# A fourth buffer for weight magnitudes, and a list schedule that keeps two engines off one PSUM tile

## The chip, the cores and the metric

The kernel runs on one core of a Trainium2 chip, as one program of 13112 instructions. The metric is the device time of one execution in microseconds (us). The median of three runs of the kernel before is 858.09 us (856.76 to 858.15).

## The reference

Chunked softmax attention, its heads joined to rows of 512, then two feed-forward layers with different activations, all in float32:

```
q, k, v: (4, 8, 576, 64), attention within chunks of 64 positions
attn = softmax(q_c @ k_c^T / 8); x = (attn @ v_c) as (2304, 512)
...
h = x @ w_in                      # layer 1: 512 -> 2048
g = max(h, 0) + log1p(exp(-|h|))  # softplus
x = g @ w_out                     # 2048 -> 512
...
h = x @ w_in2                     # layer 2, the same sizes
P = a0 + a1*h + a2*h^2 + a3*h^3
Q = 1 + |b0|*|h| + |b1|*h^2
out = (P / (Q + 1e-6)) @ w_out2
```

## The kernel before, in words

**Number format.** Each float32 operand of a large product is split into a high and a low part of type fp32r, and a product is three matmuls: high by high, high by low, low by high (`TERMS`). So each weight chunk, each x and each g is made twice, `[0]` high and `[1]` low.

**Tiles.** The 2304 tokens form five blocks (`BLOCKS`, 512 or 384 tokens), run in the order 0, 3, 4, 1, 2 in both layers. The 2048 hidden columns are 16 chunks (`fc`). One block and one chunk are a step `s`: 0 to 79 in layer 1, 80 to 159 in layer 2. A step has 12 matmuls into h (`products_h`, L824), its activation (`softplus`, L862 to L870, or `rational`, L900 to L959), and 12 matmuls in two groups of six into the accumulators (`products_out1`, L992; `products_out2`, L1022). After a block's last step `evacuate` (L1055, L1057) reads the accumulators out.

**Engines.** TensorE (PE) does the matmuls. ScalarE (ACT) does the activations and most high parts, VectorE (DVE) the low parts (L331) and arithmetic, GpSimd (POOL) other low parts (L870, L933). SyncE (SP) issues the transfers.

**Activation tables.** ACT uses one table for exponential, logarithm and Prelu (`EXP_LN`) and another for softplus (`SOFTPLUS`). `table(name)` puts an `ACT_TABLE_LOAD` (L289) into ACT's stream where the set changes.

**The first block.** During steps 0 to 15 the weights of layer 1 are converted. `convert` takes two chunks at a time, one of `w_in` (`wr_1i`, `cm_1i`, `w_1i`) and one of `w_out` (`wr_1o`, `cm_1o`, `w_1o`). `prepare` loads the raw chunk into a buffer of the pool `raw` (4 buffers, L362). ACT makes its magnitude `cm` in a buffer of the pool `cvt` (L380, 3 buffers, Prelu, table `EXP_LN`). DVE shifts it (L389) and merges bits of the raw chunk into it (L395). ACT then takes the high part (L323, no table) and DVE the low part (L331). The softplus of the same steps needs the other table, so a conversion between two steps is a switch there and one back. Meanwhile attention for later tiles runs too: `qk` and `v` are loaded, PE turns them (`qkT`, L572), makes scores, ACT the exponential (`e`, L643; `Exp`, or, where the other table is loaded, softplus of the argument less 20, of which only the ratios matter), PE the values (L696).

**Buffers that the change touches.** The pool `att1` has one buffer per tag. Its tag `v` holds the v of a tile that isn't staged (tiles 4 to 11 and 15 to 17); in layer 2, from step 80 on, it holds the scratch tile `t1` of each third step. PSUM holds two tiles `h`, two `acc`, and `att` for attention, whose room becomes `u0` and `u1` in layer 2 (`square` in `rational`). A tile `h` is read by ACT and DVE, and PE's h two steps later takes its buffer.

**What sets the order.** `Program` is a list scheduler that runs when the kernel is built. Every piece of work is a task (`add`): its engine, an estimated cost, the keys that it reads and writes, the pool tag that it allocates from (`alloc`), the table that it needs. `add` turns keys into dependencies; `alloc` keeps the allocations of one tag in the order in which they were added, and the buffers' release comes from keys with a turn number:

```
def turn(tag, bufs):
    counts[tag] = counts.get(tag, -1) + 1
    return tag, counts[tag] % bufs
```

`forward` plays the engines through in estimated time; where several tasks of an engine are ready, `pick` takes the one with the earliest latest-start time that `backward` gave. `locked` keeps DVE and POOL apart for tasks that both use the memory port. ACT puts off a task that needs the other table, if one that fits is nearly as urgent. `schedule` does this `ROUNDS` = 6 times, three of them with random shifts, and keeps the order that ends first. The tasks' instructions are then issued in that order, on each engine, as written. The costs decide the order only; on the chip each instruction waits for its semaphores.

## Time and profile before

| | |
|---|---|
| three runs, median | 858.09 us (856.76 to 858.15) |
| the profiled execution, its own time | 858.8 us |
| its span | 857.0 us |
| mean granted clock of TensorE | 0.995 |
| PE busy in the span | 842.1 us (98%) |
| DVE, ACT, POOL busy | 641.6, 506.5, 225.6 us |

The span is what the trace covers: from the first instruction to the last. The execution's own time is 1.8 us longer. A row of a timeline gives the start, the time to the end of the last instruction in it, the engine, the line, the operation, the tile written and the tiles read, the shape, how many instructions in a row it groups, and in brackets the idle time before it with what released it. The start of a PE row is recorded; the end is modelled, and so consecutive rows overlap a little. "room" stands for a wait for a buffer to become free.

### The profile page before, as it was taken

The numbers are of one execution on the slowest core, as the hardware profiler recorded it, in microseconds if no ns is written. First come the engines' busy times: TensorE is split into PE (matmuls) and PEld (weight loads), VectorE is DVE, ScalarE is ACT, GpSimd is POOL, SyncE is SP. The second block draws the span as 40 slices with busy tenths as digits, with TensorE's granted clock in tenths as the row PEclk, the third lists the DMA queues.
The fourth block names the chain that finished last, engine by engine and source line by source line (L and its number), as shares of the span: only waits on it lengthen the run. The fifth ranks groups of instructions, "written<-read, shape, count | busy, mean of one in ns | idle before, by whom it ended". The sixth has DMA issues, their size and how long they took to land.

```text
span 857.0 us, 13112 instructions
## 1 busy us (share of the span) xinstructions
PE 842.1 (98%) x5014; PEld 724.1 (84%) x5014; DVE 641.6 (75%) x1119; ACT 506.5 (59%) x875; POOL 225.6 (26%) x206
## 2 busy tenths in 40 slices
PE   7999999999999999999999999999999999999997
PEld 6878779999999888888887888889989888888885
DVE  5766778788899978316776877888878778868774
ACT  4899973233334332344448766767767767756763
POOL 0000002122212222243454821342261352213212
PEclk9899999999999999999999999999999999999999
DMA  9955433413643722235432200200210000001001
GB/s 224 247 181 176 157 99 78 95 39 85 186 123 76 210 75 74 99 119 178 144 116 86 83 1 1 87 0 1 87 50 1 37 1 1 1 0 50 1 1 49
DMA packets 76926, 71.10 MB, mean 83 GB/s; under 512 B 36160, under 2 KB 63808, under 8 KB 76864
## 3 DMA queue, kind: packets, MB, share of 16 engines
q1 hardware_dynamic: 76864, 70.27, 28.5%
q8 instruction: 39, 0.64, 0.3%
q14 instruction: 23, 0.19, 0.1%
HBM read 56.63 MB, written 13.63 MB: 82 GB/s over the span
## 4 chain that ended last, share of the span: by engine, by line
PE 75%; ACT 2%; DVE 2%; issue 0%; POOL 0%; DVEq 0%; POOLq 0%; ACTq 0%
PE h L824 37%; PE acc L1022 22%; PE acc L992 16%; DVE t L903 1%; PE aps L696 1%; ACT t L948 1%; PE aps L606 0%; DVE t L959 0%; ACT t L918 0%; ACT u L922 0%; ACT u L900 0%; ACT u L926 0%; DVE ev L1057 0%; DVE u L903 0%; POOL g L933 0%
## 5 line engine op out<-in xcount | busy, mean ns | idle before, releaser
L824 PE MATMUL h<-xT,w_1i 128*128 128x512 f32 (+1 forms) x960 | 211.1, 370 | 2.3 <-ACT w_1i L323 2.2
L992 PE MATMUL acc<-g,w_1o 128*128 128x512 f32 (+1 forms) x960 | 211.9, 369 | 0.0
L1022 PE MATMUL acc<-w_2o,g 128*128 128x512 f32 x864 | 209.9, 391 | 1.7 <-POOL g L933 0.9
L824 PE MATMUL h<-xT,w_2i 128*128 128x512 f32 (+1 forms) x960 | 210.5, 368 | 0.7 <-ACT u L900 0.4
L824 PEld LDWEIGHTS h<-xT,w_2i 128*128 128x128 f32 x960 | 175.9, 188 | 27.0 <-DVE t L903 1.3
L824 PEld LDWEIGHTS h<-xT,w_1i 128*128 128x128 f32 x960 | 173.8, 188 | 27.6 <-ACT w_1i L323 5.1
L992 PEld LDWEIGHTS acc<-g,w_1o 128*128 128x128 f32 x960 | 174.3, 188 | 23.0
L1022 PEld LDWEIGHTS acc<-w_2o,g 128*128 128x128 f32 x864 | 161.4, 188 | 35.5 <-POOL g L933 1.8
L870 POOL TENSOR_TENSOR g<-t,g 128x384 fp32r<-128x384 f32 (+1 forms) x64 | 76.2, 1191 | 344.3 <-ACT g L867 340.7
L933 POOL TENSOR_TENSOR g<-t,g 128x512 fp32r<-128x512 f32 (+1 forms) x80 | 94.6, 1182 | 250.6 <-ACT g L930 186.1
L862 ACT ACTIVATE t<-h 128x512 f32<-128x512 f32 (+1 forms) x80 | 44.3, 554 | 111.0 <-PE h L824 110.8
L903 DVE SCALAR_TENSOR_TENSOR t<-u,absb_t,t 128x512 f32<-128x512 f32 (+1 forms) x80 | 55.5, 694 | 35.6 <-ACT u L900 21.8
L867 ACT ACTIVATE g<-h 128x512 fp32r<-128x512 f32 (+1 forms) x80 | 44.3, 554 | 62.5 <-PE acc L992 58.6
L585 DVE STREAM_TRANSPOSE qkT<-qk 32x256 f32<-32x256 f32 x176 | 76.9, 437 | 4.2 <-PE aps L606 0.8
L959 DVE TENSOR_TENSOR t<-h,t 128x512 f32<-128x512 f32 (+1 forms) x80 | 50.8, 635 | 27.3 <-ACT t L918 13.6
L930 ACT ACTIVATE g<-t 128x512 fp32r<-128x512 f32 (+1 forms) x80 | 46.8, 585 | 35.0 <-DVE t L903 28.7
L922 ACT ACTIVATE u<-t,epsq_t 128x512 f32<-128x512 f32 (+1 forms) x80 | 52.0, 650 | 23.7 <-DVE t L903 21.4
L903 DVE SCALAR_TENSOR_TENSOR t<-t,epsq_t,u 128x512 f32<-128x512 f32 (+1 forms) x80 | 55.3, 691 | 13.8 <-ACT u L926 13.3
L948 ACT ACTIVATE t<-h,na_t 128x512 f32<-128x512 f32 (+1 forms) x80 | 58.5, 732 | 10.2 <-PE h L824 9.8
L900 ACT ACTIVATE u<-h 128x512 f32<-128x512 f32 (+1 forms) x80 | 43.2, 540 | 33.0 <-PE h L824 23.7
L903 DVE SCALAR_TENSOR_TENSOR t<-t,na_t,h 128x512 f32<-128x512 f32 (+1 forms) x80 | 55.5, 693 | 9.3 <-ACT u L900 3.7
L918 ACT ACTIVATE t<-h,b_t 128x512 f32<-128x512 f32 (+1 forms) x80 | 51.1, 640 | 14.7 <-PE h L824 12.1
(80 smaller groups left out, 743.7 us busy)
## 6 DMA issues: line engine op xcount, KB each, us to landing
wr_1i<-in_moe_w_in_dram SPq DMA_DIRECT2D x16, 512.0 KB, 3.9
wr_1o<-in_moe_w_out_dram SPq DMA_DIRECT2D x16, 512.0 KB, 4.5
wr_2i<-in_moe_w_in_dram SPq DMA_DIRECT2D x16, 512.0 KB, 3.9
wr_2o<-in_moe_w_out_dram SPq DMA_DIRECT2D x16, 512.0 KB, 4.1
out_dram<-ev SPq DMA_DIRECT2D x18, 256.0 KB, 2.5
qk<-in_q_dram SPq DMA_DIRECT2D x16, 256.0 KB, 5.0
qk<-in_k_dram SPq DMA_DIRECT2D x16, 256.0 KB, 5.7
v<-in_v_dram SPq DMA_DIRECT2D x16, 256.0 KB, 5.0
```

The costliest lines, as they stand in the source:

```text
L585: vec.transpose(tiles["qkT"][p0 : p0 + 32, n, :, c * CH : (c + 1) * CH].rearrange("p g (u t) -> p g t u", t=2), qk_t[tb][p1 : p1 + 32, h:: ...
L824: pe.matmul(hs[s], w[:, a, c * P : (c + 1) * P], xt[:, b, c, :n_tok], start=n == 0, stop=n == 3 * KC - 1,)
L870: (vec if by_vector else pool).tensor_tensor(out=gs[s][:, 1, :n_tok], in0=t["t2"], in1=gs[s][:, 0, :n_tok].bitcast(F32), op=ALU.subtract,)
L903: return lambda: vec.scalar_tensor_tensor(out=out(), in0=in0(), scalar=scalar, in1=in1(), op0=op0, op1=op1)
L918: act.activation(new("t1"), h(), AF.Abs, scale=b_t[:, 0:1])
L922: act.activation(u(), d(), AF.Ln, bias=epsq_t)
L930: act.activation(gs[s][:, 0, :n_tok], p(), AF.Copy)
L933: pool.tensor_tensor(out=gs[s][:, 1, :n_tok], in0=p(), in1=gs[s][:, 0, :n_tok].bitcast(F32), op=ALU.subtract,)
L948: lambda: act.activation(new("t2"), h(), AF.Identity, scale=na_t[:, 3:4], bias=na_t[:, 2:3]),
L959: lambda: vec.tensor_tensor(out=p(), in0=h(), in1=p(), op=ALU.mult), [hkey, kp], [kp],
L992: pe.matmul(accs[1, j, half][:, c % 2, :n_tok], wts[1, "o", fc][:, a, c * P : (c + 1) * P], gs[s][:, b, :n_tok], start=first and n == 0, s ...
L1022: pe.matmul(accs[2, j, half][:, c % 2], gs[s][:, b, c * P : (c + 1) * P], wts[2, "o", fc][:, a, :], start=first and n == 0, stop=last and ...
```

## The change

The planner now has a set of PSUM tiles for each task (`bank`: h, u, att or acc). `forward` keeps in `used`, for each tile, until when each engine uses it, and a task that uses the tile on another engine is started later (`when`), or another ready task is taken in its place. That works on the estimated times, and so on the order alone; the dependencies between the tasks are the same as before, but for two things. In layer 2 the squares have keys of their own (`u`) in place of `att`. And every fourth magnitude of layer 1 (`spare`) is put into the buffer of `att1` with the tag `v`, in place of one of the three of `cvt`; the load of v is therefore an allocation of that tag in the planner too. The raw buffers are four as before.

```
     def __init__(self):
-        self.tasks, self.deps, self.table, self.port = [], [], [], []
+        self.tasks, self.deps, self.table, self.port, self.psum = [], [], [], [], []
         self.writer, self.readers, self.last_alloc = {}, {}, {}
+    @staticmethod
+    def bank(key):
+        if key[0] in ("h", "u"):
+            return key
+        if key[0] == "att":
+            return "att"
+        return key[0] if isinstance(key[0], tuple) and key[0][0] == "acc" else None
...
                 deps[j] = self.tasks[j][1] + self.delay(self.tasks[j][0], engine)
-        if alloc is not None:
-            if alloc in self.last_alloc:
-                deps.setdefault(self.last_alloc[alloc], 0.0)
-            self.last_alloc[alloc] = i
+        for tag in (alloc,) if isinstance(alloc, str) else alloc or ():
+            if self.last_alloc.get(tag, i) != i:
+                deps.setdefault(self.last_alloc[tag], 0.0)
+            self.last_alloc[tag] = i
         self.tasks.append((engine, cost, fn))
...
         self.port.append(port or engine == POOL)
+        self.psum.append({self.bank(key) for key in (*reads, *writes)} - {None})
         return i
...
         until = {DVE: 0.0, POOL: 0.0}
-
-        def locked(e, i, t):
+        used = {}
+        def when(e, i, t):
             other = {DVE: POOL, POOL: DVE}.get(e)
-            return other and self.port[i] and until[other] > t + 1e-9
+            if other and self.port[i]:
+                t = max(t, until[other])
+            for tile in self.psum[i]:
+                for by, end in used.get(tile, {}).items():
+                    if by != e:
+                        t = max(t, end + self.OTHER[by])
+            return t
+        def begin(e, i, t):
+            if e in until and self.port[i]:
+                until[e] = t + self.tasks[i][1]
+            for tile in self.psum[i]:
+                used.setdefault(tile, {})[e] = t + self.tasks[i][1]
+            return i, t
...
             first = heapq.heappop(waiting)
-            if locked(e, first[1], t):
-                free = [w for w in waiting if not locked(e, w[1], t)]
+            if when(e, first[1], t) > t + 1e-9:
+                free = [w for w in waiting if when(e, w[1], t) <= t + 1e-9 and (e != ACT or fits(w[1]))]
                 if free:
...
                     heapq.heappush(waiting, first)
-                    return other[1], t
-                t = until[{DVE: POOL, POOL: DVE}[e]]
-            if e in until and self.port[first[1]]:
-                until[e] = t + self.tasks[first[1]][1]
+                    return begin(e, other[1], t)
+                t = when(e, first[1], t)
             if e == ACT and not fits(first[1]):
...
                     heapq.heappush(waiting, first)
-                    return other[1], t
+                    return begin(e, other[1], when(e, other[1], t))
                 loaded[0] = self.table[first[1]]
                 t += TABLE_LOAD
-            return first[1], t
+            return begin(e, first[1], t)
...
             ACT, 0.56 * len(parts), magnitudes, [p[0] for p in parts], [p[1] for p in parts],
-            alloc="m", table=EXP_LN if signed else None,
+            alloc=["v" if p[1] == ("v", 0) else "m" for p in parts],
+            table=EXP_LN if signed else None,
         )
...
         layer, which, fc = name
-        rkey, mkey = turn("raw", 4), turn("m", 3)
+        rkey = turn("raw", 4)
+        spare = layer == 1 and turn("spare", 4)[1] == 3
+        mkey = ("v", 0) if spare else turn("m", 3)
...
-            m = x["m", name] = cvt.tile([P, 512], F32, tag="m", name="cm_%d%s_%d" % name)
+            p, tag = (att1, "v") if spare else (cvt, "m")
+            m = x["m", name] = p.tile([P, 512], F32, tag=tag, name="cm_%d%s_%d" % name)
             up = x["r", name][:, :, 1].bitcast(F32)
...
         if not by_chunk:
-            loads["v", tb] = add(DMA, 1.2, load_v, [], [(vkey, 0)])
+            loads["v", tb] = add(DMA, 1.2, load_v, [], [(vkey, 0)], alloc=None if staged else "v")
             add(
...
                 add(PE, 0.78, scores, turned, [b0, b1], alloc=alloc)
-            add(DMA, 1.2, load_v, [], [(vkey, 0)])
+            add(DMA, 1.2, load_v, [], [(vkey, 0)], alloc="v")
         add(DVE, 0.6, maximum, [b0, b1] if by_chunk else [b0], [km], alloc="mx")
...
         t, new = scratch(s, n_tok, third)
-        ku, kp = ("att", s % 2), turn("t2", 3)
+        ku, kp = ("u", s % 2), turn("t2", 3)
         kd, kg = ((("v", 0)), "g third") if third else (turn("t1", 2), turn("g", 2))
         old = [("turned", "later", n) for n in range(16)] if third else []
+        u_keys = [("u", n) for n in range(2)]
...
         add(
-            ACT, on_act(n_tok), square, [hkey], [("att", 0), ("att", 1)] if start else [ku],
+            ACT, on_act(n_tok), square, [hkey], [*u_keys, ("att", 0), ("att", 1)] if start else [ku],
             alloc="att" if start else None,
```

What this does to the instructions of ACT, in the first block, behind the conversions of steps 1 and 2. `g_1` and `t2_1` are the two softplus readings of h of step 1, `e_12` the exponential of tile 12, `cm` a magnitude, `w` a high part. Before:

```order
L323 ACTIVATE w_1i_2_126<-cm_1i_2_480 128x512
L323 ACTIVATE w_1o_1_532<-cm_1o_1_482 128x512
L867 ACTIVATE g_1_536<-h_1_1_507 128x512
L862 ACTIVATE t2_1_547<-h_1_1_507 128x512
L643 ACTIVATE e_12_534<-e_12_534,far_t_98 128x512
L289 ACT_TABLE_LOAD
L380 ACTIVATE cm_1i_3_559<-wr_1i_3_475 128x512
L380 ACTIVATE cm_1o_2_562<-wr_1o_2_500 128x512
L289 ACT_TABLE_LOAD
L862 ACTIVATE t2_2_597<-h_1_2_569 128x512
```

Now:

```order
L345 ACTIVATE w_1i_2_126<-cm_1i_2_476 128x512
L345 ACTIVATE w_1o_1_533<-cm_1o_1_478 128x512
L311 ACT_TABLE_LOAD
L406 ACTIVATE cm_1i_3_537<-wr_1i_3_480 128x512
L406 ACTIVATE cm_1o_2_540<-wr_1o_2_501 128x512
L671 ACTIVATE e_12_535<-e_12_535 128x512
L311 ACT_TABLE_LOAD
L893 ACTIVATE g_1_579<-h_1_1_508 128x512
L888 ACTIVATE t2_1_587<-h_1_1_508 128x512
L345 ACTIVATE w_1i_3_127<-cm_1i_3_537 128x512
L888 ACTIVATE t2_2_594<-h_1_2_564 128x512
L893 ACTIVATE g_2_597<-h_1_2_564 128x512
```

The two readings of h of step 1 stood ahead of the switch for the magnitudes of step 3; they now stand behind the switch back, and behind the exponential.

ACT further on in the same block, at steps 8 and 9 (`qkT_14` is the turned q and k of tile 14, `xT_3` a part of the attention's result). Before, two pairs of magnitudes with a switch there and back each:

```order
L572 ACTIVATE qkT_14_959<-aps_14_947 128x512
L289 ACT_TABLE_LOAD
L380 ACTIVATE cm_1i_9_977<-wr_1i_9_872 128x512
L380 ACTIVATE cm_1o_8_980<-wr_1o_8_896 128x512
L572 ACTIVATE qkT_14_959<-aps_14_947 128x512
L289 ACT_TABLE_LOAD
L862 ACTIVATE t2_8_991<-h_1_8_964 128x512
L323 ACTIVATE w_1i_9_1014<-cm_1i_9_977 128x512
L867 ACTIVATE g_8_1016<-h_1_8_964 128x512
L323 ACTIVATE w_1o_8_1025<-cm_1o_8_980 128x512
L289 ACT_TABLE_LOAD
L380 ACTIVATE cm_1i_10_1031<-wr_1i_10_943 128x512
```

Now:

```order
L311 ACT_TABLE_LOAD
L406 ACTIVATE cm_1i_9_941<-wr_1i_9_837 128x512
L406 ACTIVATE cm_1o_8_944<-wr_1o_8_854 128x512
L345 ACTIVATE xT_3_703<-aps_13_732 128x4x128
L406 ACTIVATE cm_1i_10_963<-wr_1i_10_905 128x512
L406 ACTIVATE cm_1o_9_965<-wr_1o_9_930 128x512
L311 ACT_TABLE_LOAD
L888 ACTIVATE t2_8_976<-h_1_8_947 128x512
L345 ACTIVATE w_1i_9_994<-cm_1i_9_941 128x512
L598 ACTIVATE qkT_14_997<-aps_14_981 128x512
L345 ACTIVATE w_1o_8_1002<-cm_1o_8_944 128x512
L893 ACTIVATE g_8_1011<-h_1_8_947 128x512
```

Both pairs stand behind one switch. The same is so of the pairs of steps 5 and 6; the table loads of the kernel go from 31 to 27.

PE at the change of layer (the `h` of layer 2 are 80, 81, ..., `acc_1_2` the last accumulators of layer 1, halves 0 and 1). Before:

```order
L992 MATMUL acc_1_2_1_3936<-g_78_4493,w_1o_14_1360 128x512 x6
L992 MATMUL acc_1_2_0_3925<-g_78_4493,w_1o_14_1360 128x512 x6
L824 MATMUL h_2_81_4569<-xT2_0_3824,w_2i_1_4004 128x512 x12
L824 MATMUL h_2_82_4591<-xT2_0_3824,w_2i_2_4089 128x512 x12
L992 MATMUL acc_1_2_0_3925<-g_79_4534,w_1o_15_1436 128x512 x6
L992 MATMUL acc_1_2_1_3936<-g_79_4534,w_1o_15_1436 128x512 x6
L824 MATMUL h_2_83_4651<-xT2_0_3824,w_2i_3_4135 128x512 x12
L1022 MATMUL acc_2_0_0_4678<-w_2o_0_3961,g_80_4643 128x512 x6
```

Now:

```order
L1020 MATMUL acc_1_2_1_3933<-g_78_4489,w_1o_14_1340 128x512 x6
L1020 MATMUL acc_1_2_0_3922<-g_78_4489,w_1o_14_1340 128x512 x6
L850 MATMUL h_2_81_4570<-xT2_0_3821,w_2i_1_4001 128x512 x12
L1020 MATMUL acc_1_2_0_3922<-g_79_4531,w_1o_15_1423 128x512 x6
L850 MATMUL h_2_82_4609<-xT2_0_3821,w_2i_2_4086 128x512 x12
L1020 MATMUL acc_1_2_1_3933<-g_79_4531,w_1o_15_1423 128x512 x6
L850 MATMUL h_2_83_4650<-xT2_0_3821,w_2i_3_4144 128x512 x12
L1050 MATMUL acc_2_0_0_4677<-w_2o_0_3958,g_80_4663 128x512 x6
```

One half of the last accumulation, of g of step 79, now stands ahead of h of step 82, where both stood behind it.

At the end of the kernel PE's accumulations in two halves, which were interleaved one by one with the last h groups, now stand in pairs, both halves of one g together: between h of steps 156 and 157 and between those of 158 and 159 there is a pair, between 155 and 156 and between 157 and 158 nothing, where there was one group of six between each two. One group more stands ahead of the last h than before. No instruction of PE is added but for one more warm-up matmul in the start-up.

## Rows read from the trace of the kernel before

**Rows 1.** The page, busy times of the engines over the whole span.

```profile
PE 842.1 (98%) x5014; PEld 724.1 (84%) x5014; DVE 641.6 (75%) x1119; ACT 506.5 (59%) x875; POOL 225.6 (26%) x206
```

In the next view the columns are: stretch (us), its length, busy time and number of instructions of PE, PEld, DVE, ACT and POOL, PE's granted clock, the DMA engines' busy share, GB/s.

**Rows 2.** Busy times by stretch.

```profile
21.00:24.00 3.00, 3.00 (x48) 2.55 (x49) 2.60 (x5) 1.32 (x3) 0.00 (x0) 0.50 1.22 263
...
57.00:122.00 65.00, 62.46 (x358) 48.93 (x358) 47.13 (x87) 64.42 (x92) 0.00 (x0) 1.00 0.49 162
```

In the next view the columns are: waiting engine, tile and line; what released it; idle us in all, number of waits, the longest.

**Rows 3.** What PE waited for, whole span.

```profile
PE aps L667 <- DVE room L660: 2.2, 1, 2.2
PE h L824 <- ACT w_1i L323: 2.2, 5, 0.8
```

**Rows 4.** Timeline of PE, first block, the first and the last wait.

```profile
60.48 2.88 PE L992 MATMUL acc<-g,w_1o 128*128 128x512 f32 x12
63.80 3.02 PE L824 MATMUL h<-xT,w_1i 128*128 128x512 f32 x12 [0.43 <-ACT w_1i L323]
...
117.94 2.88 PE L992 MATMUL acc<-g,w_1o 128*128 128x512 f32 x12
121.62 3.72 PE L824 MATMUL h<-xT,w_1i 128*128 128x512 f32 x16 [0.80 <-ACT w_1i L323]
```

**Rows 5.** Timelines of PE, ACT and DVE at the change of layer.

```profile
452.66 5.60 PE L824 MATMUL h<-xT,w_2i 128*128 128x512 f32 x24
458.10 2.88 PE L992 MATMUL acc<-g,w_1o 128*128 128x512 f32 x12
...
460.01 0.75 DVE L903 SCALAR_TENSOR_TENSOR t<-t,na_t,h 128x512 f32<-128x512 f32 x1
...
460.79 0.58 ACT L900 ACTIVATE u<-h 128x512 f32<-128x512 f32 x1 [0.29 <-DVE t L903]
...
461.42 3.01 PE L824 MATMUL h<-xT,w_2i 128*128 128x512 f32 x12 [0.44 <-ACT u L900]
...
464.97 1.69 PE L1022 MATMUL acc<-w_2o,g 128*128 128x512 f32 x6 [0.54 <-DVE ev L1057]
```

**Rows 6.** Timelines of PE and POOL at the end.

```profile
832.26 3.02 PE L824 MATMUL h<-xT,w_2i 128*128 128x512 f32 x12 [0.25 <-DVE t L903]
835.12 5.88 PE L1022 MATMUL acc<-w_2o,g 128*128 128x512 f32 x24
...
842.63 9.59 PE L1022 MATMUL acc<-w_2o,g 128*128 128x512 f32 x41 [0.91 <-POOL g L933]
...
846.34 1.29 POOL L933 TENSOR_TENSOR g<-t,g 128x512 fp32r<-128x512 f32 x1 [1.41 <-ACT g L930]
```

In the next view the columns are: line, engine, operation, number; busy us, mean ns of one; idle us before them.

**Rows 7.** Groups of instructions of ACT, 31.8 to 121.6 us.

```profile
L289 ACT ACT_TABLE_LOAD x27 | 34.6, 1283 | 0.5
```

**Rows 8.** The page, DMA issues: number, KB each, median us to landing.

```profile
wr_1i<-in_moe_w_in_dram SPq DMA_DIRECT2D x16, 512.0 KB, 3.9
...
v<-in_v_dram SPq DMA_DIRECT2D x16, 256.0 KB, 5.0
```

**Rows 9.** Timelines of ACT, PE, DVE and SP, first block.

```profile
35.38 0.60 ACT L867 ACTIVATE g<-h 128x512 fp32r<-128x512 f32 x1
...
37.09 1.28 ACT L289 ACT_TABLE_LOAD   x1
38.38 0.66 ACT L380 ACTIVATE cm_1i<-wr_1i 128x512 f32<-128x512 f32 x1
...
37.90 2.89 PE L824 MATMUL h<-xT,w_1i 128*128 128x512 f32 x12
...
47.19 0.68 DVE L395 SCALAR_TENSOR_TENSOR cm_1i<-wr_1i,cm_1i 128x512 uint32<-128x512 uint32 x1
...
47.93 0.37 SPq L362 DMA_DIRECT2D wr_1i<-in_moe_w_in_dram  x1
...
131.80 0.68 DVE L331 TENSOR_TENSOR w_1o<-cm_1o,w_1o 128x512 fp32r<-128x512 f32 x1
...
150.74 0.69 PE L696 MATMUL aps<-aT,v 64*64 64x64 f32 x32
```

## The prediction

> **What bounds the kernel now.** I read the page's busy times first: TensorE (PE) is busy for 842.1 of 857.0 us [rows 1], so all that an edit of the order can win is PE time that is lost, 15 us at most. Then the busy times by stretch: in the first block of tokens (57 to 122 us) PE is busy for 62.46 of 65.00 us while ACT is busy for 64.42 [rows 2]. So in that block ACT sets the pace; over the whole span PE does. Then the list of what PE waited for: besides one long wait in the start-up (2.2 us) the largest is for w_1i, 2.2 us in five times [rows 3].
>
> That list undercounts, because a PE row's end is modelled and covers a short gap. I take the lost time from the starts. Twenty-four full-size matmuls from 452.66 to 458.10 us [rows 5] take 5.44 us, so twelve take 2.72, and what starts later than that was late. From 60.48 the next start should be 63.20 and is 63.80: 0.60 lost; from 117.94 it should be 120.66 and is 121.62: 0.96 lost [rows 4]. The twelve behind a wait take 2.86 us (832.26 to 835.12, [rows 6]), 0.14 more, of which I count 0.11 as the restart. Counted so from the first of these to the last, seven waits for w_1i lose 0.60, 0.21, 0.63, 0.25, 0.38, 0.39 and 0.96 us (3.42), their restarts 0.77 and one wait for aT 0.42: **4.6 us** in the first block. At the change of layer an h starts at 461.42 where 458.10 + 2.72 = 460.82 was due, and the next accumulation at 464.97 where 464.28 was due [rows 5]: with restarts **1.5 us**. At the end 0.52 us go before the last h (its wait and restart), and the last 65 matmuls or so take 16.8 us from 835.12 to 851.9 (842.63 + 41 x 0.227, [rows 6]) where 66 x 0.227 = 15.0 would do, 1.9: **2.4 us**. Sum 8.5 us, 1.0% of the span. Nothing else is there to be won, apart from the start-up, whose order the change leaves as it is.
>
> **The change, part by part.** Its first part gives layer 1's magnitudes (cm) a fourth buffer, so two pairs of them can be made behind one table switch. ACT switches its table 27 times from 31.8 to 121.6 us, 1283 ns each [rows 7]; in the new order the same steps have 23, since the pairs of steps 5 and 6 and those of steps 9 and 10 run as fours, each saving a switch there and one back. A switch blocks ACT for 1.29 us: one starts at 37.09 and the next instruction at 38.38 [rows 9]. So ACT gets 4 x 1.29 = 5.2 us back. The Trainium skill ("ScalarE: Activation LUTs", section "What ACT_TABLE_LOAD costs") puts a drain of about 1380 ns on top of the load's 1283. By it four switches would free 10.6 us; the load agrees with the row, the drain does not show.
>
> Since 5.2 is more than the 4.6 us that PE lost, ACT stops being the bound and PE becomes it: the ceiling of this part is 4.6 us. Two things are taken off. First, the new order makes g of step 1 late. Where ACT began it at 35.38 [rows 9], it now switches, makes two magnitudes (0.57 us from start to start) and the exponential of tile 12 (0.6), and switches back: 1.29 + 0.57 + 0.57 + 0.6 + 1.29 = 4.3, so g begins at about 39.7, the second reading of h ends 1.1 later at 40.8, and VectorE's low part (0.7 us) at about 41.6. PE is through with h of step 2 at 37.90 + 2.72 = 40.62 [rows 9]; of the accumulation behind it the first matmul needs only the high part, the second the low part, so from 40.85 to 41.6 PE waits anew: with a restart **0.9 us**. Second, one more warm-up matmul stands ahead of the block: 0.1 us. Left: **3.6 us**. Bounds: 4.6 if that wait is hidden, 1.8 if half of the waits for w_1i stay.
>
> The cover for this is the transfers: the raw weights still have four buffers, and one comes free only when VectorE has merged from it. A load lands 3.9 us (median) after its issue [rows 8]. For the four of steps 5 and 6 the raw tile of step 6 was issued at 47.93, as the merge of step 4 had ended (47.19 + 0.68, [rows 9]). By the new order ACT makes step 4's magnitude some 0.7 us earlier, and a DVE piece of 0.6 us no longer stands before the merge, so it goes at 46.6 and lands at 50.5, while ACT, counted on as above, wants it at about 52: 1.5 us in hand. The load of v for tile 15 shares the room now and goes out once the last magnitude is used, at the latest when VectorE was through with it before (131.80 + 0.68 = 132.5), and lands 5.0 us later at 137.5; PE wants v at 150.74 - 3.6 = 147.1 [rows 8, 9]. On SP's queue only q and k of the next tiles stand behind it, and they wait for raw buffers that the same last magnitudes free. Cost nothing; if that cover is gone, a late transfer of 2 us costs PE as much.
>
> The second part makes the planner keep ACT, DVE and PE from one PSUM tile at a time. The program had these waits already: DVE reads h until 460.76 (460.01 + 0.75), ACT's square of the same h begins at 460.79, and PE's next h, which takes that buffer, when the square has ended its read [rows 5]. So nothing is added on the chip; the order is only fitted to it. At the change of layer the new order puts one half of the last accumulation ahead of h of step 82, and ACT reads that half out before its square of h of step 81. That h ends at 452.66 + 2.72 = 455.4 in both. Then ACT has, up to and with the square, six instructions of 0.6 to 0.8 us, 3.8 in all, which end at 459.4 with 0.2 for the handover; if VectorE's second read (0.75) came only then, h is free at 460.2, and PE asks for its buffer at 455.4 + 1.36 + 2.72 + 1.36 = 460.8. The read-out, two more pieces of 0.6 and 0.7 us, ends long before 463.5, where PE wants the accumulator. Both waits go: **1.5 us** (bounds 0.5, if one half of it stays late, and 1.5).
>
> At the end the new order runs the last accumulations in pairs. Then 11 matmuls remain after the first that needs the low part of the last g, where 17 did, so the last g may come later; but the last h comes later too, as one more group of six (1.36 us) stands before it. From the end of the last h (835.12) to that of the last low part (846.34 + 1.29 = 847.63) is 12.5 us [rows 6]. Without the loss of 0.52 us before it the last h would now end at 834.60 + 1.36 = 835.96, or up to 0.5 later, since two h run back to back there and VectorE reads both; the last low part is then at 848.5 to 849.0, and PE ends 11 x 0.227 = 2.5 us after it, at 851.0 to 851.5, where it was 851.9. **0.7 us** (bounds 0 and 2.4). What follows the last matmul stays.
>
> Elsewhere PE has no wait to lose, and in the new order an h group has about as much PE work between it and the group two before it, whose buffer it takes, as in the old. Nothing.
>
> Sum: 3.6 + 1.5 + 0.7 = **5.8 us**. The profiled execution took 858.8 us (span 857.0 and 1.8 around it), which gives 853.0; the median of the runs lies 0.7 us below that execution, so I forecast 858.1 - 5.8 = **852.3 us**.
>
> **The rivals.**
> 1. *Only part of it comes.* Raw weights arrive late for the fours, or the waits for w_1i stay by half, or the planner's idea of the tiles misses at the change of layer. For it: the loads were placed for three buffers, and the hand counts leave 0.6 to 1.5 us. With half of the first part and the end alone it is 1.8 + 0.7 = 2.5 us, with the first part alone 3.6: 854.5 to 855.6.
> 2. *All of it comes.* The new wait is hidden, the end has no wait: 8.5 us, 849.6.
> 3. *A new wait drops the clock.* Behind PE's wait of 2.2 us in the start-up the granted clock is 0.50 (1.2 GHz) from 21 to 24 us [rows 2, 3]. The Trainium skill ("TensorE: Matmul & The Clock Gate", section "Part 1: The HAM clock gate (the "warmup" mystery)") says that the throttled state is the default and activity releases it, which agrees. If g of step 1 is 1.6 us later than I have it, the wait grows to 2.5 us; with 3 to 7 us at half rate (1.5 to 3.5 lost) the gain is 0.7 to 2.7 us, 857.4 at worst, no difference that can be seen. Against it: with waits up to 0.96 us the clock stayed at 1.00 from 57 to 122 us [rows 2], and 0.9 is what I expect.
> 4. *Slower: the reads of h in layer 2.* With DVE and ACT taking turns at h, a step whose h is freed late costs PE what it cost before the last h, 0.52 us. Layer 2 has 80 steps; with 11 such new waits the gain is gone, with 20 the kernel takes 862.7. For it: the planner moved instructions in nearly every step. Against it: it moved them because it now reckons with these turns.
>
> **How the numbers follow.** Forecast (4.2 to 7.4 us gained) 0.60, rival 1 0.24, rival 2 0.06, rival 3 0.05, rival 4 0.05. Within 0.2% means within 1.7 us, about what can be told here from no change. Faster: 0.60 + 0.24 + 0.06 = 0.90; within: 0.06; slower: 0.04 (part of rival 4 ends as no change). The range takes in the forecast and rival 1 with their bounds, 849.9 to 855.6 us, and leaves out the 0.16 of the others.
>
> **What would show it.** In the new profile: 23 switches before h of step 15, and that h near 118 us instead of 121.62; ACT with some 2 us of idle time from 57 to 122 us; no PE wait for w_1i over 0.3 us, one new wait of some 0.8 us for g (DVE) near 41 us; no PE wait at the change of layer; at the end still one or two waits for g from POOL. Waits for w_1i as before would prove the first part wrong, new waits for h in layer 2 the second, and a clock of 0.50 after 30 us would mean rival 3.

## The result, and the profile after

The changed kernel takes **848.61 us** (median of four runs, 848.57 to 849.11); beside it the kernel before took 858.12 us (four runs, 856.76 to 858.73). The ratio is 0.9889, 95% interval 0.9877 to 0.9901: 9.5 us faster, where 5.8 were forecast. 848.61 lies 1.3 us below the lower end of the range. The profiled execution took 848.57 us, its span is 846.8 us, 10.2 less than that of before.

The page, busy times over the whole span, to be read beside [rows 1]:

```profile
PE 836.8 (99%) x5016; PEld 723.7 (85%) x5016; DVE 636.5 (75%) x1119; ACT 501.5 (59%) x871; POOL 226.0 (27%) x206
```

What PE waited for over the whole span, the complete answer (waiting engine, tile and line; what released it; us in all, times, longest), beside [rows 3]:

```profile
PE aps L693 <- DVE room L686: 1.7, 1, 1.7
PE warm L1257 <- POOL ident masks.py:199: 1.4, 1, 1.4
PE acc L1020 <- DVE g L896: 0.7, 1, 0.7
PE aps L722 <- ACT room L715: 0.7, 1, 0.7
PE aps L632 <- ACT room L598: 0.5, 2, 0.2
PE aps L586 <- ACT room L598: 0.2, 1, 0.2
```

Behind the start-up (the five other rows lie in its first 24 us) a single wait is left in 820 us, and it is new: the one for g of step 1. No wait for w_1i, none at the change of layer and none at the end is left in this list.

Block 0: busy times of a stretch of 65 us as in [rows 2], begun 3.8 us earlier (columns as there), ACT's table loads from 30.2 to 117 us (columns as in [rows 7]), and PE's timeline at the new wait and where the h of the last steps begins:

```profile
53.20:118.20 65.00, 65.00 (x409) 52.94 (x408) 49.54 (x94) 60.93 (x90) 0.00 (x0) 1.00 0.49 162
...
L311 ACT ACT_TABLE_LOAD x23 | 29.5, 1283 | 0.4
...
39.18 0.45 PE L1020 MATMUL acc<-g,w_1o 128*128 128x512 f32 x1
40.34 1.43 PE L1020 MATMUL acc<-g,w_1o 128*128 128x512 f32 x5 [0.71 <-DVE g L896]
...
116.82 7.07 PE L850 MATMUL h<-xT,w_1i 128*128 128x512 f32 x36
```

ACT is busy for 60.93 us of 65, not for 64.42 [rows 2], so it has 4.1 us to spare where some 2 were forecast; PE is busy for all of it. The first matmul of the accumulation of step 1 stands at 39.18, the second at 40.34 in place of 39.41: 0.93 lost, and 0.11 more for the restart. The h of step 15 begins at 116.82, where it was 121.62 [rows 4].

The change of layer and the end, PE's timeline, and the last low part on POOL:

```profile
455.36 2.88 PE L850 MATMUL h<-xT,w_2i 128*128 128x512 f32 x12
458.07 1.52 PE L1050 MATMUL acc<-w_2o,g 128*128 128x512 f32 x6
459.44 2.88 PE L850 MATMUL h<-xT,w_2i 128*128 128x512 f32 x12
...
825.45 2.88 PE L850 MATMUL h<-xT,w_2i 128*128 128x512 f32 x12
828.17 14.03 PE L1050 MATMUL acc<-w_2o,g 128*128 128x512 f32 x60
...
838.06 1.29 POOL L961 TENSOR_TENSOR g<-t,g 128x512 fp32r<-128x512 f32 x1 [2.08 <-ACT g L958]
```

Each row starts 2.71 to 2.72 us behind a row of twelve and 1.37 behind the row of six, so nothing is lost between them [rows 5, 6 show the waits that stood here]. No wait for a g from POOL is left at the end, where one or two were forecast.

The start-up, by stretch, first of the kernel before, then of the changed one (columns as in [rows 2]):

```profile
24.00:26.00 2.00, 2.00 (x65) 1.88 (x62) 0.80 (x2) 2.00 (x5) 0.00 (x0) 0.50 1.09 295
```

```profile
19.50:22.50 3.00, 2.48 (x39) 2.36 (x40) 3.00 (x10) 1.34 (x3) 0.00 (x0) 0.50 1.11 350
24.00:26.00 2.00, 1.96 (x43) 1.70 (x32) 1.53 (x4) 2.00 (x6) 0.00 (x0) 1.00 1.11 336
```

The granted clock is 0.50 from 19.6 to 26.4 us before, and from 19.5 to 22.9 after, and PE's first h starts at 26.87 us, not at 28.32.

**Where the 10.2 us come from.** I take every two matmuls that follow each other, subtract the usual distance of their starts (0.227 us for 512 columns, 0.173 for 384, 0.111 for 128), and add up what is left, by stage:

| stage | before | after | gained | forecast |
|---|---|---|---|---|
| start-up: PE's first h starts at | 28.32 | 26.87 | 1.45 | 0 |
| block 0: lost | 5.05 | 1.37 | 3.68 | 3.6 |
| change of layer: lost | 1.57 | -0.04 | 1.61 | 1.5 |
| end, from 820 us: lost | 2.52 | 0.23 | 2.29 | 0.7 |
| the rest: small waits and restarts in layers 1 and 2, the last read-out | | | 1.2 | 0 |

Reckoned instead between points at which PE has the same matmuls behind it in both kernels (121.96 us before and 117.05 after, 465.31 and 458.30, and so on), block 0 gives 3.5, the change of layer 1.55, the end 2.3 and the rest 1.4 us: a stage sum is good to some 0.2 us.

### The profile page after: what moved, and what is told of

Same layout as the page of the kernel before. It is cut to its first block, busy times and chain, and to the rows that moved or that the text cites. A ratio compares the mean times of both kernels' runs of the same rounds, so it can differ in the third digit from the quotient of the medians.

```text
span 846.8 us, 13140 instructions
## 1 busy us (share of the span) xinstructions
PE 836.8 (99%) x5016; PEld 723.7 (85%) x5016; DVE 636.5 (75%) x1119; ACT 501.5 (59%) x871; POOL 226.0 (27%) x206
## 4 chain that ended last, share of the span: by engine, by line
PE 96%; DVE 1%; ACT 1%; DMA 1%; issue 0%; POOL 0%; POOLq 0%; SPq 0%; DVEq 0%; ACTq 0%
PE h L850 46%; PE acc L1020 23%; PE acc L1050 23%; PE aps L632 1%; PE aps L722 1%; DMA wr_1o<-in_moe_w_out_dram 1%; PE aps L586 1%; PE warm L1257 0%; ACT L311 0%; DVE sm L675 0%; DVE room L686 0%; DVE mx L650 0%; DVE room L659 0%; ACT cm_1o L406 0%; PE aps L693 0%
```

## The experiments

Times are medians; each ratio is to the kernel before on the same chip. In all of them the stage sums are made as above.

| kernel | us | ratio, 95% interval | first h at | lost in block 0 | change of layer | end |
|---|---|---|---|---|---|---|
| buffer alone | 858.10 | 0.9993 to 1.0011 | 27.53 | 6.1 | 1.6 | 2.5 |
| exclusion alone | 854.22 | 0.9941 to 0.9971 | 29.82 | 5.6 | 0.0 | 0.2 |
| new order to 130 us alone | 853.33 | 0.9931 to 0.9958 | 26.88 | 1.1 | 1.7 | 2.5 |
| end: PE as before | 851.12 | 0.9899 to 0.9929 | 25.93 | 4.6 | 0.0 | 1.2 |
| end: the others as before | 851.66 | 0.9913 to 0.9940 | 26.88 | 1.9 | 0.0 | 2.5 |
| buffer alone, seed 3 | 857.30 | 0.9981 to 1.0005 | 26.08 | 1.9 | 1.5 | 0.7 |
| whole change, seed 5 | 853.09 | 0.9925 to 0.9955 | 27.88 | 4.1 | 0.7 | 0.0 |
| whole change, seed 3 | 849.15 | 0.9878 to 0.9911 | 28.22 | 0.8 | 0.0 | 0.0 |

### Each part alone

Buffer alone:

```
         def when(e, i, t):
...
-            for tile in self.psum[i]:
-                for by, end in used.get(tile, {}).items():
-                    if by != e:
-                        t = max(t, end + self.OTHER[by])
             return t
```

> The changed kernel with its fourth buffer, but with a planner that takes no notice of PSUM tiles; 29 table loads in all. Theory (each stage's gain belongs to one part: block 0 to the buffer, start-up, change of layer and end to the planner): the first block gains 3 to 3.7 us, PE's first h starts near 28.3 us as before, the waits at the change of layer (1.6 us) and at the end (2.3 us) are back: 854.4 to 855.1 us. Rival (the buffer shifts all later work and so also clears the other waits): about 849 us.

Exclusion alone: `spare = False` in `prepare`.

> The changed kernel with three magnitude buffers as before, and the planner that keeps engines off one PSUM tile; 31 table loads. Theory: the waits for w_1i in the first block stay (4.6 us), those at the change of layer and at the end go (3.9 us together): 854.2 us, give or take 1.5 us for the start-up, in which this order differs from both kernels (it has 12 warm-up matmuls in PE's waits there). Rival (the buffer does it all): 858 us.

The second came as the theory had it. The first gained **nothing**, since block 0 lost 6.1 us in other waits, where it had lost 5.05. What ACT waited for from 28 to 122 us, and PE, with the buffer alone:

```profile
ACT cm_1i L402 <- DMA wr_1i<-in_moe_w_in_dram: 1.6, 1, 1.6
ACT qkT L594 <- PE aps L582: 0.8, 2, 0.6
ACT cm_1o L402 <- DMA wr_1o<-in_moe_w_out_dram: 0.7, 1, 0.7
```

```profile
PE aps L582 <- ACT qkT L594: 2.6, 2, 1.8
...
PE acc L1046 <- POOL g L957: 0.9, 1, 0.9
```

This order puts its one four-fold conversion at steps 4 and 5, where the raw weights are still on their way; ACT stands still, and PE waits for qkT, which comes behind. So the two switches that it saves (25 from 28 to 122 us in place of 27) are given back. It is rival 1's first mechanism, raw weights that arrive late. The changed kernel has its fours at steps 5 and 6 and at 9 and 10, and in its profile ACT waited 0.2 us for raw weights in this stretch.

### The stages one by one

One kernel holds both orders of the same tasks (`apart`: the changed kernel's, `plain`: without the exclusion) and goes over from one to the other at a planned time:

```
+        apart, plain = prog.both()
+        order = prog.switch(apart, plain, 130.0)
```

> The changed kernel, in the planner's new order up to 130 us, and from there on in the order that it finds when it takes no notice of PSUM tiles. Theory (the stages' gains are apart from each other): the first block keeps its 3.7 us, the waits at the change of layer (1.6 us) and at the end (2.3 us) are back, with up to 1 us of small ones: 852.5 to 853.5 us. Rival (the later waits went because the work of block 0 was done sooner): under 850 us.

853.33 us, and stage for stage the theory: block 0 keeps its gain, 1.7 and 2.5 us are lost again later. The gains are apart from each other and add up.

For the end, the same from 800 us on, for some engines alone:

```
+        order = prog.weave(prog.switch(apart, plain, 800.0, (PE,)))
...
+        order = prog.weave(prog.switch(apart, plain, 800.0, (ACT, DVE, POOL)))
```

> The changed kernel; in the last 40 us PE in the order of before (accumulations one by one between the last h groups), the other engines in the new one. Theory (the end's gain is that ScalarE and VectorE have one g less left at the last h, 11.2 us of work instead of 12.5): up to 1.2 us more than the changed kernel, 848.6 to 849.8 us. Rival (the gain is PE's pairs, 11 matmuls behind the last low part in place of 17): all 2.3 us are back, 850.9 us.

> The changed kernel; in the last 40 us ScalarE, VectorE and GpSimd in the order of before, PE in the new one. Theory (the end's gain is the other engines' shorter work behind the last h): 12.5 us from the last h to the last low part, then 11 matmuls: 1.2 us or more above the changed kernel, 849.8 to 851 us. Rival (the gain is PE's pairs): no more than 0.3 us above, 848.6 to 848.9 us.

The times of both are blurred by block 0 (next section); by its time alone, 851.12 us, the first would speak for its rival. So the stage sums decide: with PE's old order 1.2 us are lost at the end, 1.0 more than in the changed kernel; with the others' old order 2.5, all that the change had gained. PE's timelines there, first with PE as before, then with the others as before:

```profile
826.59 3.03 PE L893 MATMUL h<-xT,w_2i 128*128 128x512 f32 x12
829.46 11.50 PE L1093 MATMUL acc<-w_2o,g 128*128 128x512 f32 x49
841.26 4.15 PE L1093 MATMUL acc<-w_2o,g 128*128 128x512 f32 x17 [0.31 <-POOL g L1004]
```

```profile
821.69 3.01 PE L893 MATMUL h<-xT,w_2i 128*128 128x512 f32 x12 [1.02 <-DVE t L974]
824.54 2.88 PE L1093 MATMUL acc<-w_2o,g 128*128 128x512 f32 x12
827.26 2.88 PE L893 MATMUL h<-xT,w_2i 128*128 128x512 f32 x12
829.98 5.87 PE L1093 MATMUL acc<-w_2o,g 128*128 128x512 f32 x25
836.76 8.23 PE L1093 MATMUL acc<-w_2o,g 128*128 128x512 f32 x35 [0.91 <-POOL g L1004]
```

PE's pairs alone don't bring it; they ask for their h sooner, and with ACT and DVE as before PE waits for DVE's read and for the low part of a g. The order of the other engines carries the larger share (1.3 us without PE's), and PE's fits it. Neither half keeps the length that its theory gave it: from the last h to the last low part it is 11.7 us with PE as before and 11.8 with the others as before, in place of 11.2 and 12.5.

### The start-up, and the wait for g of step 1

In the start-up the new order has DVE divide tile 1's exponentials (`room_1`) ahead of the sum of tile 2's. The move was made alone in the kernel before (first line), and undone alone in the changed one (second line):

```
+        order = prog.put(order, [mark["divide", 1]], before=mark["total", 2])
...
+        order = prog.put(order, [mark["divide", 1]], behind=mark["total", 2])
```

> The kernel before, with the one instruction moved: in the start-up the division of tile 1's exponentials ahead of the sum of tile 2's. Theory: 1.4 us less than before, 856.7 us, PE's first h near 26.9 us, clock 0.50 for some 3.4 us. Rival 1: 0.6 less, 857.5 us. Rival 2 (ScalarE, which bounds block 0, doesn't start earlier): no change, 858.1 us.

> The kernel before, with nothing but the one instruction moved (in the earlier run of this name the waits at the change of layer had changed too, which took 1.6 us away). Theory now: the move makes PE's wait in the start-up 0.6 us shorter (2.46 to 1.86 us), and how long the clock stays at 0.50 behind it differs from execution to execution whatever the order: 0.6 us less than before, 857.5 to 858.0 us. Rival (the shorter wait also halves the stretch at 0.50): 1.4 us less, 856.7 to 857.2 us.

> The changed kernel, with one instruction of VectorE moved back to where it stood before: in the start-up the division of tile 1's exponentials stands again behind the sum of tile 2's. Theory (this one move gave the start-up's gain, 0.6 us through the division and the rest through a shorter stretch at clock 0.50): 850.0 us, PE's first h near 28.3 us instead of 26.87, clock 0.50 for some 6.8 us instead of 3.4. Rival 1 (the clock's shorter stretch has another cause): 849.2 us, 0.6 more. Rival 2 (the start-up's gain is lost again behind ScalarE in block 0): 848.6 us.

The first try took 856.07 us (0.9956 to 0.9981), but it also issued the engines' instructions in another sequence to each other (`weave`), and its waits at the change of layer were gone too. The second differs from the kernel before in the one move alone: 856.68 us (0.9978 to 0.9995), 1.4 us by the medians, with 0.4 to 1.9 as its interval, the rival's number and not the theory's. PE's wait shrinks by 0.6 us in both executions that were profiled (2.25 to 1.65 us).

The clock differs from execution to execution. In the profiles here a mean granted clock of 0.994 to 0.996 goes with a stretch of 6.8 us at 0.50 behind that wait (part of it in [rows 2]), 0.997 or 0.998 with one of 3.4 us there (in two profiles at 42 us instead), 0.999 or 1.00 with none. A mean of 0.995 was shown by 16 of the 30 runs of the kernel before in these two experiments; with the early division by none of the 11 runs of the second try, and by one of the 6 of the first (0.994, and the whole 6.8 us in its profile). The runs of before at a mean of 1.00 took 855.92 to 856.65 us. So the long stretch is rarer behind the shorter wait, but it is not gone.

The first try shows something else. On every engine its instructions stand in the order of before, but for that one of DVE, and yet PE loses nothing at the change of layer, where the second try loses 1.6 us. ACT's and DVE's reads of h of step 80, before and in the first try, with PE's timeline there:

```profile
451.42 1.28 ACT L289 ACT_TABLE_LOAD   x1
452.71 0.69 ACT L918 ACTIVATE t<-h,b_t 128x512 f32<-128x512 f32 x1
453.43 0.69 DVE L959 TENSOR_TENSOR t<-h,t 128x512 f32<-128x512 f32 x1 [5.00 <-ACT t L918]
```

```profile
451.01 0.69 DVE L987 TENSOR_TENSOR t<-h,t 128x512 f32<-128x512 f32 x1 [3.01 <-ACT u L928]
...
452.52 0.69 ACT L946 ACTIVATE t<-h,b_t 128x512 f32<-128x512 f32 x1 [0.24 <-DVE t L931]
...
457.67 2.88 PE L1020 MATMUL acc<-g,w_1o 128*128 128x512 f32 x12
460.39 2.88 PE L852 MATMUL h<-xT,w_2i 128*128 128x512 f32 x12
```

DVE's instruction uses nothing that L918 writes; both read the same tile h. Before, it stands behind L918 and so behind the table load; in the first try it goes first and ACT waits for it, and PE's next h starts 2.72 us behind its accumulations, with both halves of the last accumulation where they were. So here the sequence in which two engines were issued at a shared tile changed the waits, with neither engine's own order changed.

With the move undone the changed kernel took 850.21 us (848.86 to 851.69), as forecast, yet not as argued: in its profile the clock never fell in the start-up and the first h started at 25.78. The time went in block 0 instead, ACT's waits (28 to 122 us), PE's timeline and the stretches:

```profile
ACT cm_1o L433 <- DMA wr_1o<-in_moe_w_out_dram: 1.6, 2, 0.9
...
ACT cm_1i L433 <- DMA wr_1i<-in_moe_w_in_dram: 1.2, 1, 1.2
```

```profile
40.77 0.50 PE L1048 MATMUL acc<-g,w_1o 128*128 128x512 f32 x1 [2.00 <-ACT g L921]
41.98 0.80 PE L1048 MATMUL acc<-g,w_1o 128*128 128x512 f32 x1 [0.71 <-DVE g L924]
...
42.00:44.00 2.00, 2.00 (x5) 1.62 (x6) 1.96 (x5) 1.98 (x4) 0.00 (x0) 0.50 0.41 87
```

PE comes sooner, the raw weights for the magnitudes ahead of g don't, PE waits 2.2 and 1.0 us by the starts, and the clock falls to 0.50 behind it. This is rival 3, in one execution; the kernel with PE's old end shows the same (4.6 us lost in block 0). Both have the changed kernel's order in block 0 on each engine, but both were issued in another sequence (`weave`), and no run separates that from chance. Four more runs of the changed kernel tell how often it meets this:

> The changed kernel unchanged, for the spread of its times beside the next three. Where the clock does not drop in the start-up, PE reaches the accumulation of step 1 about 1 us sooner, while g of step 1 waits behind magnitudes whose raw weights are still on their way: PE then waits 2 us and more there and the clock drops behind it. Theory: times from 848.6 to 851.7 us, the median above 848.6. Rival (the waits in the kernels with one part undone were those parts' own): all within 0.3 us of 848.6.

848.92 us (848.26 to 849.36): the ends the theory named were not reached, so the changed kernel as it was issued hardly meets this. I then filled PE's wait with small matmuls into a free bank:

```
+        def keep_busy(n):
+            for _ in range(n if tb == 1 else 0):
+                pe.matmul(bank(1)[:, :P], ident, ident, start=True, stop=True)
...
         def turn_e():
+            keep_busy(6)
```

> The changed kernel with 17 more small matmuls in the two waits of PE's start-up (12 ahead of the turning of tile 1's exponentials, 5 ahead of its values), into a bank of PSUM that is free there. Theory: the clock stays at 1.00 through the start-up in every execution, PE's first h starts near 25.9 us, and then the wait for g of step 1 grows as it does where the clock stays up by itself: 849 to 851.7 us, no better than the changed kernel. Rival (the start-up's time is kept): 847.6 us.

> The changed kernel with 6 small matmuls (12 instructions of 0.11 us, 1.3 us) in PE's first wait of the start-up, which is 1.65 us long, so that none comes late. Theory (how long the clock stays at 0.50 hangs on that wait): no stretch at 0.50 behind it in the profile, PE's first h near 26 us in every execution; the time as in the changed kernel's executions without such a stretch, 848.2 us. Rival (the clock's stretch has nothing to do with the wait): 0.50 from some 20 us on in the profile, 848.7 us.

The first kernel had 12 and 5 of them, twice what fits (each runs as two instructions): the clock stayed at 1.00, but PE came late, first h at 27.94; 849.45 us (849.29 to 849.99). With 6 the stretch at 0.50 is gone as well, the first h starts at 25.54, and the time is 848.11 us (847.78 to 849.45):

```profile
19.50:22.50 3.00, 2.43 (x76) 1.83 (x72) 3.00 (x9) 1.94 (x4) 0.00 (x0) 1.00 1.13 339
```

The mean clock was 0.999 or 1.00 in all four runs. That agrees with the theory but does not prove it, for the changed kernel run again had no stretch at 0.50 in its profile either, with its wait of 1.66 us unfilled. Of the 1.33 us that the first h is earlier than in the changed kernel's profile, 0.7 come out at the end of that profile; block 0 loses 0.7 more. Lastly, the wait for g of step 1:

```
+        order = prog.put(order, [mark["hi", 1], mark["whole", 1]], before=mark["magnitudes", 1, ("i", 3)])
...
+        order = prog.put(order, [mark["lo", 1]], before=mark["shift", (1, "i", 3)])
+        order = prog.put(order, [mark["whole", 2], mark["hi", 2]], before=mark["split", wkey[1, "i", 3]])
```

> The changed kernel with the two readings of h of step 1 ahead of the table switch again, where they stood before; nothing else moved. Theory (the new wait for g of step 1 costs 1.0 us, and more where PE comes earlier): 847.6 us, no PE wait for g near 40 us, and no execution above 849 us. Rival (the magnitudes of step 3, 1 us later now, become the wait): no change, 848.6 us.

> As the kernel with the readings of h of step 1 ahead of the switch, now on all engines: VectorE's low part of that g ahead of the shift for step 3, and ScalarE's readings of h of step 2 ahead of the high part of w_1i of step 3, which waited 1.4 us there. Theory: PE's wait near 40 us (1.0 us) goes and no other comes: 847.7 us. Rival (ScalarE has no time to spare at that place, a wait for w_1i of step 3 or for qkT takes its place): 848.7 us or more.

> Both. Theory: 847.2 us (the start-up's steady clock counts once g of step 1 is not waited for). Rival: 848.2 us or more.

The first line alone gave 849.98 us: DVE's low part had stayed behind the merges of step 3, and PE waited 1.33 us. All three gave 848.46 us (847.99 to 849.58), with the matmuls 848.20, the earlier version with all 17 matmuls and the first line 850.26, where 846.6 was forecast. PE's waits with all three lines moved, in the slowest of its four executions:

```profile
PE aps L615 <- ACT qkT L627: 1.7, 1, 1.7
...
PE h L879 <- ACT w_1i L373: 0.4, 1, 0.4
```

The wait for g goes and others come, so the 1 us is not won. That ACT has no time to spare there agrees with it, but one profile does not show it.

### Another seed

The planner starts from random shifts. Three kernels change the seed alone (`SEED, SHAKEN = 3, 3` or `5, 3`):

> The changed kernel with its fourth buffer and a planner that takes no notice of PSUM tiles, but with another seed of its random shifts (3 in place of 2). Its order has 27 table loads, as the changed kernel's, one half of the last accumulation ahead of h of step 82, and the division of tile 1 early. Theory (the gains belong to the order that a search happens to find, not to PSUM tiles being kept apart): well below the same kernel with seed 2 (858.1 us), 849 to 854 us. Rival (PSUM tiles have to be kept apart): 857 us or more.

> The changed kernel with seed 5: 33 table loads in all, both halves of the last accumulation behind h of step 82, the division of tile 1 late, as before. Theory (the order found decides): the change of layer and the start-up lose what they lost before (1.6 and 0.6 to 1.4 us), and the first block is bound by ScalarE's switches: 853 to 858 us. Rival (keeping PSUM tiles apart is what gains): under 850 us.

> The changed kernel with seed 3: 23 table loads in all, half of the last accumulation ahead of h of step 82, the division early. Theory (PE is the bound once ScalarE has some time to spare, so fewer switches bring no more than the wait for g of step 1): 847.5 to 849 us. Rival (each switch less still brings 1.3 us): 844 us.

The times are 857.30, 853.09 and 849.15 us: the first speaks for the rival, the second for the theory, the third is just above its theory's range, and the stages say why. Block 0 goes with the order that is found: the buffer alone loses only 1.9 us there with seed 3, and the whole change 4.1 with seed 5. Layer 2 goes with the exclusion: with it the change of layer loses 0.7 us or less in all three seeds, and the time from 470 to 820 us comes out within 0.2 us of the changed kernel's; without it seed 3 loses 1.5 us at the change of layer and, between 470 and 820 us, 3.7 us more than seed 2 does. The place of the half accumulation does not decide this: the buffer alone with seed 3 has one half ahead of h of step 82 and loses the 1.5 us, the whole change with seed 5 has both behind it and loses 0.7. PE's waits in the buffer alone with seed 3:

```profile
PE acc L1046 <- DVE ev L1081: 3.8, 2, 2.6
...
PE h L846 <- DVE t L927: 1.0, 3, 0.4
```

DVE reads accumulators out late there, at the change of layer and after the next block, and PE wants them. The whole change with seed 3 has four switches less still and loses 0.6 us less in block 0, where PE has hardly a wait left to lose. Its first h starts 1.35 us later: against what its expectation says, the trace has the division of tile 1 late, behind the sum (17.84 and 18.44 us), with PE's wait at 2.25 us and the clock at 0.50 for 6.8. No version here is clearly faster than the changed kernel. The kernel before and the exclusion alone were not run with another seed, so it is not shown that the gain in block 0 needs the buffer.

## Why the prediction was wrong

Its direction and the numbers of its two largest steps held. Block 0: 3.6 us forecast, 3.7 measured, the new wait for g of step 1 among it (0.9 forecast near 41 us with its restart, 0.93 and 0.11 found at 40.3), 23 switches as counted, 1283 ns each. The change of layer: 1.5 forecast, 1.6 measured. The other three terms were too small: the end, and the start-up and the rest, which stood at nothing. (The range's lower end, 849.9 us, does not follow from the largest gain named beside it, 7.4 us, which gives 850.7; the result lies below both.)

- **The end**, forecast 0.7, measured 2.3. The step that failed is "From the end of the last h (835.12) to that of the last low part is 12.5 us", carried over into the new order. It is 11.2 us there (828.17 to 838.06 + 1.29), since ACT and DVE have three g left to finish at the last h, where four were left. I had moved PE's rows and left the other engines' as they were; the run with the others' old order loses the whole 2.3.
- **The start-up**, forecast nothing, since "whose order the change leaves as it is". PE's rows were the same, DVE's weren't. The division that PE waits for stands one instruction of 0.6 us earlier, and the stretch at clock 0.50 behind that wait, 6.8 us in the profile of before, is 3.4 us in that of after. The 0.6 us belong to the order; the stretch differs from run to run and is only rarer. Moved alone the division gave 1.4 us by the medians (interval 0.4 to 1.9).
- **Elsewhere**, forecast nothing, 1.2 us in sum: a wait of 0.27 us for aT at 167 us and two restarts in layer 2 went, the rest is spread over thousands of matmuls; no run tells more.

Three arguments have less behind them than I thought:

- **The buffer.** That "ACT stops being the bound" is no property of the buffer: alone, with the same seed, it gained nothing, and rival 1 (raw weights late) was then the case, not a 24% outsider. The 3.7 us went with the place at which this search put the fours, so that number was in part luck.
- **The half accumulation.** "Nothing is added on the chip" was to the point, and rival 4 did not come; in the changed kernel the square of h of step 81 ends 4.3 us behind that h, where 4.0 were counted. But that the 1.5 us come from one half standing ahead of h of step 82 is not shown: with both halves behind it the first try of the early division loses nothing there and the change with seed 5 only 0.7 us, and with one half ahead of it the buffer alone with seed 3 loses 1.5. No run moved the half alone.
- **The clock.** Rival 3 did not come in the two profiles of the changed kernel, but two profiles of other kernels with the same order in block 0 show the clock fall behind the wait for g.

## What to carry to other kernels

When a schedule is found by a search, compare the order on **every** engine in every stage where the bounding engine waits, and not its own rows alone: here some 2.7 of the 9.5 us came from rows of VectorE and ScalarE. Compare also which engine is issued first at a tile that two of them use: that alone took 1.6 us of waits away. Price a chain of work by what is left in the queues at its start, not by its length in the old order. And test such an edit with several seeds: what stays with all of them belongs to the edit, the rest to the search.

## What was not expected of the hardware

Whether the clock falls behind a wait is not settled by the wait's length in these profiles. Behind PE's start-up wait of 2.25 us it fell to 0.50 in four of five profiles (6.8 us in three, 3.4 in one), behind the same wait at 1.65 us in five of ten (6.8 us in one, 3.4 in four), and in none of the four kernels that filled that wait with small matmuls. In block 0 it fell behind waits of 2.0 and 0.7 us with one matmul between them and behind 1.4 and 0.7, and stayed at 1.00 behind one of 1.76 us with the buffer alone. The runs of before with a mean clock of 1.00 took some 2 us less than those with 0.995.
